# Batch 0's first k and v parts moved to ScalarE's DMA queue, and the last unit's products put into another order of banks and stores

## The chip, the cores and the metric

The kernel runs on one core of one Trainium2 chip. The metric is the device time of one execution in microseconds (us); the median of several executions is quoted. A *profile* is one execution taken by the hardware profiler; its *span* is some 1.8 us shorter than the device time of the same execution. PE is the TensorE matmul, PEld its weight load, DVE the VectorE, ACT the ScalarE, POOL the GpSimd and SP the SyncE.

Two kinds of number appear, and they must not be mixed. The *timed* numbers say what the change is worth. The *profiled* ones say where the time goes; each is one execution.

## The reference, cut to what matters

```python
q_p, k_p = phi(q), phi(k)                      # phi(x) = elu(x) + 1; q, k, v: 8 x 8 x 576 x 64, f32
kv  = einsum('bhsd,bhse->bhde', k_p, v)
out = einsum('bhsd,bhde->bhse', q_p, kv) / den # linear attention
x   = out as (4608, 512)
for e in range(4):                             # four experts, w1: 512 x 1024, w2: 1024 x 512, f32
    y += p[:, e:e+1] * (relu(x @ w1[e]) @ w2[e])
```

The kernel works in 36 units, nine tiles of 512 tokens by four experts. Eight tiles are one batch's first 512 tokens each; the ninth gathers the remaining 64 tokens (the *remainders*) of all batches. Most matmuls use a Strassen-like scheme with seven products where eight would be needed.

## The kernel before: the parts that matter

All of batch 0's loads are issued by SyncE, in one order. A part is 256 KB; `load_left` issues a remainder as two DMAs of 64 KB.

```python
ORDER = [(n, 2 * g + i) for g in range(2) for n in "qkv" for i in range(2)]
...
homes = ["h"] * 4 + [None] * NRAW + ["u2", "u3"]
for (n, i), home in zip(ORDER, homes):
    b0.load(n, i, home=home)                # q0 q1 k0 k1 [k rest] v0 v1 [v rest] q2 q3 k2 k3 v2 v3
    if i == 1 and n != "q":
        b0.load_left(n)
load_probs(nc.sync, True)
```

POOL issues the expert weights. In its program order that comes after the cast of the v remainder (`'lv'`), and part of it after a piece of phi of k3 (`'kd3'`):

```python
"START": (11, 'qa0', 'ka0', 'kd0', 'qa1', 'lka', 'qd0', 'lv', 6, ..., 'dma0', ..., 'kd3', ..., 'dma1', ...)
```

The last unit of all computes seven products, each for two blocks of 128 tokens, into two PSUM banks (`b` as `run`, `e` as `side`), and DVE adds each result to an accumulator. Product 3 needs POOL's last hidden sum:

```python
order = L2ORD if n < len(units) - 1 else (2, 1, 5, 6, 3, 7, 4)   # banks: e b e b e b b
...
if (j, e) == (NTILES - 1, E - 1):
    if p in (3, 7, 4):       # 3: whole rows of block i; 7 and 4: the two halves of block 2 + i
        store(j, ns, {3: slice(0, Dm), 7: c2, 4: c1}[p], True)
```

A store is two DMAs, one on SyncE's and one on ScalarE's queue, so this is six stores on each.

## Time and profile before

| what | value |
|---|---|
| time, median | 499.92 us (4 runs, 499.61 to 500.02) |
| profiled span | 498.2 us |
| PE busy | 97% of the span |
| batch 0's hardware-queue packets | 3.42 MB, from 1.85 to 14.56 us |
| POOL issues the first weights | 10.76 us |
| first store to the end of the span | 490.99 to 498.18 us |

The page, the parts on busy time and on the chain that ended last:

```profile
PE 483.7 (97%) x4343; PEld 408.5 (82%) x4343; DVE 378.1 (76%) x800; ACT 337.3 (68%) x680; POOL 357.5 (72%) x339
PE 83%; ACT 6%; DVE 4%; DMA 3%; POOL 1%; issue 1%; POOLq 0%; SPq 0%; ACTq 0%; DVEq 0%
```

In the middle PE is the limit, and neither half of the change touches the middle. Two places are left. The first is the start. The windows view gives, for each stretch, busy us and count of each engine, then the granted clock, the DMA share and GB/s:

```profile
core 0: us, PE busy (x) PEld busy (x) DVE busy (x) ACT busy (x) POOL busy (x), PEclk, DMA share, GB/s
2.00:6.00 4.00, 4.00 (x12) 1.49 (x11) 0.49 (x1) 0.65 (x2) 1.91 (x1) 1.00 0.97 289
6.00:10.00 4.00, 3.52 (x21) 1.51 (x18) 2.94 (x9) 3.48 (x7) 0.00 (x0) 1.00 0.89 270
13.00:20.00 7.00, 6.29 (x63) 3.89 (x61) 6.35 (x21) 5.72 (x15) 6.98 (x9) 1.00 1.35 187
26.00:34.00 8.00, 6.51 (x35) 2.99 (x34) 2.72 (x5) 3.35 (x6) 2.86 (x4) 1.00 1.14 218
```

The DMA engines are occupied from 2 us on, first by batch 0, then by weights. Between 26 and 34 us PE is busy for only 6.51 of 8 us. The view of waits of that stretch says why (waited for in total, times, longest):

```profile
DVE s L603 <- DMA w<-in_moe_w_dram: 9.2, 1, 9.2
PEld L731 <- DMA w<-in_moe_w_dram: 2.0, 2, 1.5
PE pe L731 <- DMA w<-in_moe_w_dram: 1.0, 1, 1.0
```

In the timeline these four lines tell the story of the start (start us, duration, engine, line, operation; in brackets the idle time before and what ended it):

```profile
7.70 0.40 ACT L353 ACTIVATE el<-rl 128x256 f16<-128x256 f32 x1
10.21 0.40 POOL L357 CAST vl<-rl 128x256 f16<-128x256 f32 x1 [4.67 <-DMA rl<-in_v_dram]
10.76 3.34 POOL L182 DMA_DIRECT2D w<-in_moe_w_dram  x4 [0.15 <-issue]
33.57 0.61 PE L731 MATMUL pb<-tt,s 128*128 128x256 f16 x4 [0.43 <-DVE s L605]
```

They are the exp of the k remainder, the cast of the v remainder, the first weight issue, and the first product that uses DVE's sum of weights. The last is a milestone that I call M.

The second place is the tail:

```profile
489.56 1.33 PE L666 MATMUL pe<-w,hs 128*128 128x256 f16 x8
490.05 0.55 PEld L666 LDWEIGHTS <-hs 128*128 128x128 f16 x6 [0.39 <-POOL hs L639]
490.99 3.77 SPq L555 DMA_DIRECT2D out_dram<-acc  x6
491.00 4.35 ACTq L555 DMA_DIRECT2D out_dram<-acc  x6
492.53 0.92 DVE L568 SCALAR_TENSOR_TENSOR acc<-pb,p_sb,acc 128x256 f32<-128x256 f32 x2 [0.25 <-PE pb L666]
```

PE waits inside product 3 for POOL, the stores run back to back on both queues (a `q` after the engine's name marks issuing), and DVE's last pair of adds waits for PE.

### The profile page before, as it was taken

To read this page: it belongs to the slowest core of one execution; us is meant where nothing else is said; L and a number is where in the kernel's file an instruction comes from. 1 tells how busy PE (TensorE), PEld (TensorE's weight loads), DVE (VectorE), ACT (ScalarE), POOL (GpSimd) and SP (SyncE) were. 2 spreads that over 40 slices of the span, in tenths; PEclk is the share of its full clock that TensorE was granted. 3 is DMA by queue.
4 is the path that set the end of the run, shared out by engine and by line. 5 is a ranking of instruction groups with operands and counts; after the bars stand their busy time and mean duration, and the time that the engine had idled before them with its cause. 6 is when DMAs were issued, how large, how long until landed. Compare 5 with 4: busy or idle time off the path is not lost.

```text
span 498.2 us, 11603 instructions
## 1 busy us (share of the span) xinstructions
PE 483.7 (97%) x4343; PEld 408.5 (82%) x4343; DVE 378.1 (76%) x800; ACT 337.3 (68%) x680; POOL 357.5 (72%) x339
## 2 busy tenths in 40 slices
PE   8989989899999999999999999999999999999995
PEld 3546756789898989898989898989898888888884
DVE  5647898788876988598869886888687756775685
ACT  5857969974987488847894789568954565446530
POOL 3734304878977697769776977698669877987773
PEclk9999999999999999999999999999999999999999
DMA  8999974642454234632454245523231020002002
GB/s 244 200 215 246 271 150 124 207 113 57 109 167 128 62 95 144 157 75 76 142 167 84 57 153 147 101 52 95 86 79 29 5 94 1 1 1 86 1 1 86
DMA packets 81880, 53.65 MB, mean 108 GB/s; under 512 B 46176, under 2 KB 75360, under 8 KB 81824
## 3 DMA queue, kind: packets, MB, share of 16 engines
q1 hardware_dynamic: 71520, 41.12, 30.5%
q0 software_dynamic: 9824, 11.27, 12.1%
q8 instruction: 34, 0.56, 0.5%
q10 hardware_dynamic: 480, 0.52, 0.3%
q14 instruction: 22, 0.18, 0.1%
HBM read 45.16 MB, written 9.44 MB: 110 GB/s over the span
## 4 chain that ended last, share of the span: by engine, by line
PE 83%; ACT 6%; DVE 4%; DMA 3%; POOL 1%; issue 1%; POOLq 0%; SPq 0%; ACTq 0%; DVEq 0%
PE py L666 37%; PE pb L731 23%; PE pe L731 17%; DMA w<-in_moe_w_dram 3%; PE py L577 2%; PE psum_kv L423 1%; PE psum_nd L463 1%; DMA rawh<-in_k_dram 1%; ACT u L742 1%; ACT vp L330 1%; ACT psum_ee L314 1%; DVE t L622 1%; DVE h L715 1%; DVE acc L568 1%; ACT h L757 1%
## 5 line engine op out<-in xcount | busy, mean ns | idle before, releaser
L568 DVE SCALAR_TENSOR_TENSOR acc<-py,p_sb,acc 128x256 f32<-128x256 f32 (+1 forms) x382 | 182.6, 488 | 46.4 <-PE py L666 40.1
L715 DVE CUSTOM_DVE_ANT_0 h<-pe,u 128x512 f16<-128x512 f32 x140 | 96.3, 688 | 46.9 <-PE pe L731 25.4
L731 PEld LDWEIGHTS <-w 128*128 128x128 f16 x1120 | 108.6, 98 | 18.4 <-DMA w<-in_moe_w_dram 2.0
L633 POOL TENSOR_TENSOR hs<-h 128x512 f16<-128x512 f16 x64 | 74.3, 1160 | 56.1 <-DVE h L715 55.0
L666 PEld LDWEIGHTS <-h 128*128 128x128 f16 x1024 | 99.6, 98 | 12.8 <-issue 1.4
L666 PE MATMUL py<-w,h 128*128 128x256 f16 x744 | 106.4, 273 | 0.5 <-ACT acc L566 0.5
L742 ACT COPY u<-pb 128x512 f32<-128x512 f32 x140 | 82.7, 591 | 27.5 <-PE pb L731 26.3
L635 POOL TENSOR_TENSOR hs<-hs,h 128x512 f16<-128x512 f16 x64 | 73.9, 1155 | 27.7 <-PE py L666 25.1
L731 PEld LDWEIGHTS <-s 128*128 128x128 f16 x840 | 81.5, 98 | 13.4 <-issue 1.1
L731 PE MATMUL pb<-tt,w 128*128 128x256 f16 x560 | 84.1, 273 | 0.5 <-ACT u L742 0.5
L666 PEld LDWEIGHTS <-hs 128*128 128x128 f16 x768 | 74.3, 98 | 9.1 <-POOL hs L639 0.4
L639 POOL TENSOR_TENSOR hs<-h,hs 128x512 f16<-128x512 f16 x64 | 74.4, 1162 | 3.6 <-PE py L666 3.1
L666 PE MATMUL py<-t,hs 128*128 128x256 f16 x496 | 74.4, 273 | 0.0
L637 POOL TENSOR_TENSOR h<-h 128x512 f16<-128x512 f16 x64 | 74.4, 1162 | 0.0
L757 ACT ACTIVATE h<-pe 128x512 f16<-128x512 f32 x70 | 41.9, 598 | 47.1 <-PE pe L731 46.6
L751 ACT COPY pe<-pb 128x512 f32<-128x512 f32 x70 | 40.2, 574 | 41.4 <-PE pb L731 14.8
L775 ACT ACTIVATE h<-pb 128x512 f16<-128x512 f32 x70 | 41.9, 599 | 8.8 <-PE pb L731 8.7
L731 PE MATMUL pb<-tt,s 128*128 128x256 f16 x280 | 42.0, 273 | 0.4 <-DVE s L605 0.4
L731 PE MATMUL pe<-tt,s 128*128 128x256 f16 x280 | 42.0, 273 | 0.0
L731 PE MATMUL pe<-xT,w 128*128 128x256 f16 x248 | 37.2, 273 | 1.0 <-DMA w<-in_moe_w_dram 1.0
L731 PE MATMUL pe<-xT,s 128*128 128x256 f16 x248 | 37.2, 273 | 0.9 <-DVE h L715 0.9
L731 PE MATMUL pb<-xT,w 128*128 128x256 f16 x248 | 37.2, 273 | 0.1
(120 smaller groups left out, 607.6 us busy)
## 6 DMA issues: line engine op xcount, KB each, us to landing
out_dram<-acc SPq DMA_DIRECT2D x32, 256.0 KB, 2.5
w<-in_moe_w_dram POOLq DMA_DIRECT2D x14, 512.0 KB, 12.1
rawb<-in_v_dram SPq DMA_DIRECT2D x26, 256.0 KB, 2.7
rawb<-in_q_dram SPq DMA_DIRECT2D x26, 256.0 KB, 2.8
rawb<-in_k_dram SPq DMA_DIRECT2D x26, 256.0 KB, 3.2
w<-in_moe_w_dram POOLq DMA_DIRECT2D x4, 256.0 KB, 6.6
rawb<-in_k_dram POOLq DMA_DIRECT2D x4, 256.0 KB, 10.1
rl<-in_q_dram SPq DMA_DIRECT2D x16, 64.0 KB, 2.5
```

The source lines that it names most:

```text
L568: nc.vector.scalar_tensor_tensor(out=acc, in0=ps, scalar=pscal, in1=acc, op0=AO.mult, op1=AO.add)
L633: nc.gpsimd.tensor_tensor(out=hs[0], in0=a21, in1=a22, op=AO.add)
L635: nc.gpsimd.tensor_tensor(out=hs[1], in0=hs[0], in1=a11, op=AO.subtract)
L637: nc.gpsimd.tensor_tensor(out=a21, in0=a11, in1=a21, op=AO.subtract)
L639: nc.gpsimd.tensor_tensor(out=hs[3], in0=a12, in1=hs[1], op=AO.subtract)
L666: nc.tensor.matmul(out=ps, lhsT=lhsT(k), rhs=rhs[:, k], start=first and k == 0, stop=k == FH - 1, skip_group_check=True,)
L715: nc.vector._custom_dve(TENSOR_ADD_SAT, out=out, in0=ps, in1=u, s0=BIG, s1=0.0)
L731: nc.tensor.matmul(out=ps[:, kk], lhsT=lk(kc), rhs=rhs[:, kc], start=first and kk == 0 and kc == 0, stop=kc == 1, skip_group_check=True,)
L742: nc.scalar.copy(u, self.b)
L751: nc.scalar.copy(self.e5, self.b)
L757: nc.scalar.activation(self.h[:, :, 0, 0:NH], self.e5, AF.Relu)
L775: nc.scalar.activation(self.h[:, :, 1, 0:NH], self.b, AF.Relu)
```

## The change

The intent at the start is that q and k arrive side by side and SyncE gets to the later parts sooner. In the last unit it is to take PE's two gaps away: product 3 comes later, behind POOL's last sum, and successive products alternate between the banks, so that product 4 no longer waits for the bank that product 7 has just filled. The stores become four whole-row ones per queue. The diff, cut at `...`, without the parts that are not used (other placements that the list allows); the remarks after `#` are mine:

```diff
+    "B0": ('sq0', 'sq1', 'ak0', 'ak1', 'slk', 'av0', 'av1', 'slv', 'sq2', 'sq3', 'sk2', 'sk3', 'sv2', 'sv3'),
...
-        homes = ["h"] * 4 + [None] * NRAW + ["u2", "u3"]
+        homes = dict(sq0="h", sq1="h", sk0="h", ...)   # the same buffers, now by name
-        for (n, i), home in zip(ORDER, homes):
-            b0.load(n, i, home=home)
-            if i == 1 and n != "q":
-                b0.load_left(n)
+        for x in CFG["B0"]:                      # s: SyncE's queue, a: ScalarE's
+            eng = {"s": nc.sync, "a": nc.scalar, "p": nc.gpsimd}[x[0]]
+            if x[1] == "l":
+                b0.load_left(x[2], eng=eng)
+            else:
+                b0.load(x[1], int(x[2]), eng, homes.get(x))
...
         if (j, e) == (NTILES - 1, E - 1):
-            if p == 2:                           # the first product takes the two banks
+            if p == 1:
...
-        if (j, e) == (NTILES - 1, E - 1):
-            if p in (3, 7, 4):
-                store(j, ns, {3: slice(0, Dm), 7: c2, 4: c1}[p], True)
-        elif e == E - 1 and p in (3, 4):
-            store(j, ns)
+        if e == E - 1 and p in (3, 4):
+            store(j, ns, j == NTILES - 1)
...
-            order = L2ORD if n < len(units) - 1 else (2, 1, 5, 6, 3, 7, 4)
+            order = L2ORD
+            if n == len(units) - 1:
+                order, at = (1, 2, 6, 5, 7, 3, 4), at + NSLOT      # banks: b e b e b e b
```

More of the change, by code (lines that the diff above doesn't have):

```diff
@@ L544, in new_py, with store @@
         return ppm.tile([P, Dm], FP32, tag="py", bufs=2, name="py")
-    def store(j, ns, ds=slice(0, Dm), last=False):
-        acc = accs[j, ns][:, ds]
+    def store(j, ns, last=False):
+        acc = accs[j, ns]
         if j < B:
@@ L555, in store @@
                 (nc.scalar if last and u else nc.sync).dma_start(
-                    out=out_b[2 * ns + u, SM:S, ds],
+                    out=out_b[2 * ns + u, SM:S],
                     in_=acc[u * HP : (u + 1) * HP],
@@ L794, in unit @@
         return layer1(j, e, hT, phs) + layer2(j, e, hT)
-    ORDER = [(n, 2 * g + i) for g in range(2) for n in "qkv" for i in range(2)]
     def order_of(at):
@@ L870 @@
         b0.alloc_left()
-        homes = ["h"] * 4 + [None] * NRAW + ["u2", "u3"]
-        for (n, i), home in zip(ORDER, homes):
-            b0.load(n, i, home=home)
-            if i == 1 and n != "q":
-                b0.load_left(n)
+        homes = dict(sq0="h", sq1="h", sk0="h", sk1="h", ak0="h", ak1="h", pv0="hs1", pv1="hs1", sv2="u2", sv3="u3")
+        for x in CFG["B0"]:
[4 more added lines that the diff above has]
+                b0.load(x[1], int(x[2]), eng, homes.get(x))
         load_probs(nc.sync, True)
@@ L886 @@
             "lv": (b0.left_v, nc.gpsimd),
+            "V2": (b0.load, "v", 2, nc.gpsimd, "hs3"),
+            "V3": (b0.load, "v", 3, nc.gpsimd, "hs3"),
             "dma0": (load_first, 0, 4),
@@ L899, with gate @@
             steps[f"ph{i}"] = partial, i
+        dump = pconst.tile([P, 1], FP32, tag="dump", name="dump")
+        def gate(n, i):
+            nc.gpsimd.tensor_copy(out=dump, in_=b0.raw[n, i][:, 0, 0, 0:1])
+        for n in "qkv":
+            for i in range(4):
+                steps[f"g{n}{i}"] = gate, n, i
         turn["aps"] = list(CFG["APS"])
```

## The prediction

> **What bounds it.** PE is busy 97% (page, part 1) and heads the chain of waits with 83%. Only the ends are not PE-bound: between 30 and 34 us PE loses 1.4 us (windows) while DVE waits 9.2 us and PE 1.0 us for weights (view of waits), and after 490 us the kernel drains.
>
> *Start.* The hardware queue carries batch 0 from 2 to 14 us at 264-311 GB/s, DMA share 0.88-1.02 (windows); the software queue with the weights is saturated from 14 to past 34 us (share 1.1-1.4). SyncE issues a 256 KB part in 0.46 us, a 64 KB remainder in 0.6-0.75 (timeline). Landings, from what ended waits: q0 3.55, k0 6.10, v0/v1 9.5, v remainder 10.2. POOL waits 4.7 us for that remainder and issues weights only at 10.76.
>
> *Tail.* POOL's last sum ends at 489.99 and holds product 3 back by 0.39 us; product 4 reuses product 7's bank and waits 0.31 us (timeline). The last DVE add ends 493.45. But ScalarE's six stores run back to back from 491.00, 0.5-0.8 us each, the last issued at 494.87, 1.4 us after its data; SyncE's last at 494.22. Data moves until about 496.5; the span ends at 498.2.
>
> **What the change does.** Work is the same. Start: k0, k1, v0, v1 move to ScalarE (4 x 0.5 us of issue before its 1.28 us table load, so ready near 4.1 us). Estimates from 290 GB/s shared equally: q0 3.55 -> 4.1, k0 6.1 -> 4.3, k1 and q1 near 5.7, v0/v1 9.5 -> 8.9, v remainder 10.2 -> 8.3. So POOL issues weights up to 2 us earlier. The Trainium skill, "DMA: Bandwidth & Descriptors", section "Issuing engines are not separate DMA queues", says several issuers only save issue time, as the same 16 engines carry all; this trace agrees so far, with a share of 0.9-1.0 from 2 us on. So the wait for weights near 31 us shrinks only by the idle share of the first 12 us and a better overlap of two queues: 0.3-1.0 us. Against it, earlier weights interleave with k3, v2, v3, which may land 1 us later. Net start: 0.5 us gained (estimate).
>
> Tail: order 1,2,6,5,7,3,4 puts product 3 behind the last sum, and gives product 4 the bank freed longer before. Both PE gaps (0.39 + 0.31) go; last add near 492.9 (0.55 earlier). Eight half-row stores (64 KB) become four full-row ones (128 KB): four issues per queue, the last near 493.6 (estimate) instead of 494.87, but twice as large. The same 1.05 MB drains at about 285 GB/s from a start 0.6 us later. Net tail: 0.6 us gained.
>
> All of it is critical, but is 1.1 of 500 us. Predicted 498.7 us, eight times in ten between 497.7 and 499.9; faster by over 2%: 0.01, within 2%: 0.98, slower by over 2%: 0.01.
>
> **What would show it.** Two hardware queues in the first 10 us; first exp of k0 near 4.7 instead of 6.13; POOL's cast of the v remainder near 8.5 instead of 10.21; first weight issue near 9; PE's wait near 31 us shorter and earlier. Last unit: no PE gap before products 3 and 4, four stores a queue. Middle unchanged.
>
> **What would make it wrong.** The weight stream's end may not move (purely rate-bound), leaving the tail; late v2/v3 may stall PE near 16-20 us; SyncE may stall where a remainder's semaphore must come free first; full-row stores may land later than they are issued earlier; or two queues may run clearly faster together, giving 2 us.

## The result and the profile after

498.35 us median (498.26 to 498.93, 4 runs) against 499.92: 1.6 us less. The ratio is 0.9972 with a 95% interval of 0.9955 to 0.9989. Ratios here are the mean time of one kernel's fast runs over that of the other's of the same rounds, so not quite the ratio of the medians quoted. Below 2% it counts as the same speed, but it is clear of 1. Two more timings of the same code gave 0.9964 (0.9950 to 0.9978) and 0.9989 (0.9977 to 1.0000). The last interval touches 1. So 0.5 to 1.8 us is what the runs support. Executions in which one die ran at a lower clock are left out of the means.

The profiled execution was the slowest of the four, with a span of 497.2 us. The windows of the start:

```profile
core 0: us, PE busy (x) PEld busy (x) DVE busy (x) ACT busy (x) POOL busy (x), PEclk, DMA share, GB/s
2.00:6.00 4.00, 4.00 (x15) 1.64 (x14) 1.54 (x3) 2.85 (x4) 1.76 (x1) 1.00 1.00 323
6.00:10.00 4.00, 3.19 (x17) 1.22 (x15) 1.29 (x4) 1.30 (x4) 0.15 (x1) 1.00 1.16 270
13.00:20.00 7.00, 6.26 (x63) 3.92 (x60) 6.14 (x19) 6.64 (x17) 6.98 (x9) 1.00 1.33 183
26.00:34.00 8.00, 7.84 (x45) 4.12 (x43) 3.49 (x7) 4.78 (x9) 3.16 (x5) 1.00 1.15 217
```

Batch 0 moved faster at first (323 instead of 289 GB/s), and PE is now busy for 7.84 of the 8 us from 26 to 34. The view of waits there has no PE wait for weights any more, and DVE's is 2 us shorter:

```profile
DVE s L604 <- DMA w<-in_moe_w_dram: 7.2, 1, 7.2
PEld L729 <- DVE s L606: 0.3, 1, 0.3
```

The four lines of the story, by the timeline:

```profile
9.40 0.42 ACT L354 ACTIVATE el<-rl 128x256 f16<-128x256 f32 x1 [2.70 <-DMA rl<-in_k_dram]
10.01 0.40 POOL L358 CAST vl<-rl 128x256 f16<-128x256 f32 x1 [3.86 <-DMA rl<-in_v_dram]
10.57 3.39 POOL L183 DMA_DIRECT2D w<-in_moe_w_dram  x4 [0.16 <-issue]
32.80 0.61 PE L729 MATMUL pb<-tt,s 128*128 128x256 f16 x4
```

This is not what I had pictured. The remainders did not come earlier: k's exp is 1.7 us later, v's cast 0.2 us earlier. PE's attention work ends 1.19 us *later* than before. Yet M is 0.77 us earlier. The tail:

```profile
490.57 2.48 SPq L556 DMA_DIRECT2D out_dram<-acc  x4
490.58 2.84 ACTq L556 DMA_DIRECT2D out_dram<-acc  x4
490.94 0.92 DVE L569 SCALAR_TENSOR_TENSOR acc<-pb,p_sb,acc 128x256 f32<-128x256 f32 x2
```

The last pair of adds ends at 491.86, 1.59 us earlier, but the span ends only 1.01 us earlier. PE's instruction stream is the same in both kernels up to the last unit, so the two traces can be laid side by side, instruction by instruction. After minus before: 1.19 us later in the attention, 0.78 earlier at M, 0.55 from 48 us on, and exactly 1.00 from 152 us to the first product of the last unit. The jump of 0.45 near 151 us has nothing to do with any line that was changed. In the timeline of before it is this wait of PE, for ScalarE's first sum into an accumulator:

```profile
150.76 0.60 PE L731 MATMUL pb<-xT,w 128*128 128x256 f16 x4
151.84 0.60 PE L666 MATMUL py<-w,h 128*128 128x256 f16 x4 [0.47 <-ACT acc L566]
```

and after, where the gap is short and ScalarE's own wait is put down to the store that must free the accumulator:

```profile
150.31 0.47 ACT L567 ACTIVATE acc<-py,p_sb 128x256 f32<-128x256 f32 x1 [0.57 <-DMA out_dram<-acc]
150.84 0.60 PE L667 MATMUL py<-w,h 128*128 128x256 f16 x4
```

So the first pair of traces left three questions: is the gain the start's or the tail's, is the 0.45 us near 151 us part of it, and why is a later attention faster?

### The profile page after: what moved, and what is told of

The parts are those of the page before. It is cut to its first block, busy times and chain, and to the rows that moved or that the text cites. A ratio compares the mean times of both kernels' runs of the same rounds, so it can differ in the third digit from the quotient of the medians.

```text
span 497.2 us, 11596 instructions
## 1 busy us (share of the span) xinstructions
PE 482.3 (97%) x4343; PEld 408.8 (82%) x4343; DVE 378.2 (76%) x800; ACT 337.5 (68%) x680; POOL 358.0 (72%) x339
## 4 chain that ended last, share of the span: by engine, by line
PE 82%; DMA 7%; ACT 5%; DVE 3%; POOL 2%; issue 1%; SPq 0%; POOLq 0%; ACTq 0%
PE py L667 38%; PE pb L729 22%; PE pe L729 17%; DMA rawb<-in_k_dram 2%; DMA rl<-in_k_dram 2%; PE py L578 1%; PE psum_nd L464 1%; PE psum_kv L424 1%; DMA rl<-in_v_dram 1%; ACT psum_ee L315 1%; DVE acc L569 1%; ACT u L740 1%; DVE t L623 1%; DMA rawh<-in_q_dram 1%; POOL w L183 1%
## 5 line engine op out<-in xcount | busy, mean ns | idle before, releaser
L667 PE MATMUL py<-w,hs 128*128 128x256 f16 x248 | 37.2, 273 | 0.0
```

Source lines behind the costliest of these rows:

```text
L667: nc.tensor.matmul(out=ps, lhsT=lhsT(k), rhs=rhs[:, k], start=first and k == 0, stop=k == FH - 1, skip_group_check=True,)
```

## The experiments

Twelve runs, in three groups of four; the kernels of a group shared a chip and the runs of the kernel before. All results were correct.

| run | what it is | median us | before, same rounds | ratio (95%) |
|---|---|---|---|---|
| a1 | start alone | 498.36 | 500.06 | 0.9961 (0.9946-0.9976) |
| a2 | tail alone | 499.73 | 500.06 | 0.9992 (0.9977-1.0007) |
| a3 | changed kernel again | 498.41 | 500.06 | 0.9964 (0.9950-0.9978) |
| a4 | remainders first | 500.60 | 500.06 | 1.0005 (0.9989-1.0021) |
| b1 | weights issued early | 500.83 | 499.90 | 1.0020 (1.0006-1.0033) |
| b2 | changed, old stores | 498.03 | 499.90 | 0.9962 (0.9950-0.9975) |
| b3 | changed, old order | 497.98 | 499.90 | 0.9969 (0.9953-0.9986) |
| b4 | kernel before again | 499.58 | 499.90 | 0.9995 (0.9982-1.0009) |
| c1 | changed kernel, third time | 498.82 | 499.78 | 0.9989 (0.9977-1.0000) |
| c2 | as b2 | 498.53 | 499.78 | 0.9978 (0.9966-0.9989) |
| c3 | as b3 | 498.18 | 499.78 | 0.9983 (0.9964-1.0003) |
| c4 | changed, only k moved | 498.34 | 499.78 | 0.9977 (0.9965-0.9989) |

### a1 to a3: the halves apart

a1 is the changed kernel with before's order, banks and stores of the last unit; a2 is before with the new ones; a3 is the changed kernel once more.

```diff
 a1, from the changed kernel              a2, from the kernel before
-order, at = (1, 2, 6, 5, 7, 3, 4), ...   -(2, 1, 5, 6, 3, 7, 4)
+order = (2, 1, 5, 6, 3, 7, 4)            +(1, 2, 6, 5, 7, 3, 4), bank pair taken at product 1
-store(j, ns, j == NTILES - 1)            -store(j, ns, {3: ..., 7: c2, 4: c1}[p], True)
+store(j, ns, {3: ..., 7: c2, 4: c1}[p], True)  +store(j, ns, j == NTILES - 1)
```

> Only the queues of batch 0's loads change; the last unit is as before. Theory A (the gain is mostly at the start: the two queues together move batch 0 about 11% faster, so the weight stream begins and ends earlier): 0.8 to 1.2 us less than before, PE 0.7 to 0.9 us earlier at 33 us though the attention is 1.2 us later. Theory B (the gain is mostly the tail, and the 0.5 us that the first trace shows near 150 us is chance): 0.3 to 0.6 us less.

> Only the last unit changes (order, banks, full-row stores). Theory A: the last DVE add comes 0.59 us earlier in its unit, but the stores also begin 0.6 us later, so the end moves by 0 to 0.3 us. Theory B: 0.6 to 1.0 us less than before.

> The changed kernel once more beside its two halves: 1.3 to 1.7 us less than before. If the halves add up, start plus tail should give this within 0.3 us. The profile tells whether the 0.46 us near 150 us, which the first trace showed as gained, is gained again.

Measured: 498.36 for the start alone, 498.41 for both, on the same chip. The tail alone is not told apart from before (0.9992, interval across 1). Theory A holds and B falls: the start has the whole gain, and more than the 0.8 to 1.2 us expected by the medians (1.7). a2's profile shows both sides of the tail. Its last add comes 6.80 us after the unit's first product, where before's comes 7.39 us after it, as expected 0.59 earlier; yet from the first product to the end of the span it is 12.12 us, and 12.11 before.

### b4: was the wait near 151 us chance?

> The kernel before once more, with a profile: 0 +- 0.3 us. It tells whether the wait of 0.46 us at PE near 150 us belongs to that kernel or to one execution: by chance, it is gone or shorter here, and the profiled span is then 0.4 to 0.6 us below the first one's 498.2.

The code is the kernel before, unchanged. Its time is 499.58, its profiled span 497.4 instead of 498.2, and the gap is gone:

```profile
150.67 0.60 PE L731 MATMUL pb<-xT,w 128*128 128x256 f16 x4
151.11 0.60 PE L666 MATMUL py<-w,h 128*128 128x256 f16 x4
```

So 0.45 of the 1.00 us by which the first pair of profiles differed ahead of the last unit was one execution's luck. In c2, a variant of the *changed* kernel, PE's gap at the same instruction is 0.40 us, and none is left in a1 or a2. This is why I give M and the last unit as means of several profiles. M is 33.57, 33.47 and 33.69 us in the three profiles with before's start (before, b4, a2), mean 33.58. In the eight with the new start (after, a1, a3, b2, b3, c1, c2, c3) it is 32.32 to 32.80, mean 32.45. That is 1.13 us. The last unit's first product differs by 1.06 us over the same profiles (485.65 and 484.59). What is gained at M arrives at the end.

### c4: how much has to be moved?

```diff
-"B0": ('sq0', 'sq1', 'ak0', 'ak1', 'slk', 'av0', 'av1', 'slv', 'sq2', ...
+"B0": ('sq0', 'sq1', 'ak0', 'ak1', 'slk', 'sv0', 'sv1', 'slv', 'sq2', ...
```

> The changed kernel with v0 and v1 back on SyncE's queue, so that only k0 and k1 go by ScalarE. Theory A (the gain is what the two queues together save in draining batch 0): about half of the overlap remains, the last hardware packet comes near 13.6 us, PE at 33 us is 0.4 to 0.7 us ahead of before instead of 1.0, and the time is 0.3 to 0.6 us above the changed kernel. Rival (the gain is k0 and k1 landing early, so ScalarE and DVE start sooner): no loss, within 0.2 us of the changed kernel.

Theory A, in the form "so much overlap, so much gain", fell: with half as much on ScalarE's queue nothing is lost. 498.34 stands against 498.82 for the changed kernel on the same chip, and M is 32.23. The last packet of batch 0 comes at 13.08 us, where half the gain would have given 13.6. The rival guessed the time but not the reason. k0 and k1 do land early in both kernels. But the attention is 0.6 us earlier than in the first profile of before here and 0.7 to 1.2 us later in the changed kernel, and the time hardly tells. Here PE waits for weights again, as it did in before, only sooner:

```profile
PEld L729 <- DMA w<-in_moe_w_dram: 1.0, 1, 1.0
PEld L729 <- DVE s L606: 0.9, 1, 0.9
```

So M is not set by the same thing in the two kernels. Measure it from N, the start of the attention's last four products `psum_nd`. Here are N in before, in the changed kernel and in c4, and then M in c4:

```profile
18.19 0.39 PE L463 MATMUL psum_nd<-kvz,qT 128*128 128x130 f16 x4 [0.23 <-ACT kvz L439]
19.38 0.39 PE L464 MATMUL psum_nd<-kvz,qT 128*128 128x130 f16 x4 [0.32 <-ACT kvz L440]
17.59 0.39 PE L464 MATMUL psum_nd<-kvz,qT 128*128 128x130 f16 x4 [0.33 <-ACT kvz L440]
32.23 0.61 PE L729 MATMUL pb<-tt,s 128*128 128x256 f16 x4 [0.43 <-DVE s L606]
```

From N to M it takes 15.38 to 15.84 us in the three profiles with before's start, 14.64 in c4, and 13.39 to 13.50 in the eight with the changed start. In a4, below, where PE waits for nothing on the way, it takes 13.40. So waiting for weights cost before 2.0 to 2.4 us, costs c4 1.2 and the changed kernel at most 0.1. The changed kernel is no longer held up by weights at M: its late attention sets M and gives back a part of what the earlier weights won. That c4 and the changed kernel come out so close is in part chance.

What the two kernels share is the end of batch 0's hardware packets: 14.56, 14.09 and 14.27 us in the three profiles with before's start, 13.14 to 13.68 in the eight with the changed start, 13.08 here. The first megabyte of weights, as the packets count it, is complete at 19.09 to 19.53, at 18.01 to 18.74, and at 17.98 us.

c4 also points to what delayed the attention. With v0 and v1 behind the k remainder on SyncE's queue, its exp starts at 6.96 us; with them on ScalarE's, at 8.88 to 9.40. In the changed kernel, in the single microsecond from 6 to 7, the DMA view reads:

```profile
q10 hardware_dynamic: 222, 0.22, 80.3%
q1 hardware_dynamic: 253, 0.06, 30.8%
```

q10 is ScalarE's queue, q1 SyncE's (packets, MB, share of 16 engines' time). In this microsecond the counts are alike, as if the two queues took turns packet by packet. But SyncE's packets were the remainders' small ones, so it moved 0.06 MB against 0.22. Equal turns are shown for this microsecond only: in the one before SyncE's queue moved 93 packets and ScalarE's 283, in the one after 675 and 84.

### a4: the remainders first

```diff
-"B0": ('sq0', 'sq1', 'ak0', 'ak1', 'slk', 'av0', 'av1', 'slv', 'sq2', ...
+"B0": ('sq0', 'ak0', 'slk', 'slv', 'ak1', 'sq1', 'av0', 'av1', 'sq2', ...
```

> The changed kernel with both remainders issued right after the first q part, q1 behind k1. Theory S (the 64 KB remainders with their 256-byte packets are starved beside ScalarE's 1 KB packets): POOL's cast of the v remainder moves from 10.0 to 6 to 8 us, weights are issued 2 us earlier, the k remainder's exp moves from 9.4 to about 7. If the weight stream is bound by its rate and total, its end moves by less than 0.3 us and the time stays within 0.3 us of the changed kernel; if it is bound by when it is first issued, the time falls by another 1 to 2 us.

A miss that taught something: 500.60 us, 2.2 more than the changed kernel on the same chip. The v remainder's cast came at 8.80 us (6 to 8 expected), so POOL issued the first weights at 9.14 instead of 10.1 to 10.6. The first weight packet moved at 13.03 us all the same, just when batch 0 was through (last packet 13.31). Issuing earlier bought nothing. Taken alone this looks as if the weights had to wait for batch 0; b1, below, refutes that. On the other side q1 now stood behind the remainders in SyncE's queue, and SyncE issued it at 5.65 us, after gaps of 0.8 and 0.9 us in its issuing, where the program has it wait for earlier DMAs whose semaphores it uses again. Its first use on ScalarE came at 9.30 us, after 4.00 us of waiting for it; the k remainder's exp, which follows it there, came at 10.36 (about 7 expected), and PE's attention was 2.36 us later than in before. Now PE was the limit at M, not the weights:

```profile
33.95 0.60 PE L729 MATMUL pb<-tt,s 128*128 128x256 f16 x4
```

No wait of PE for weights is left between 26 and 34 us. Once the weights no longer hold PE up, each further delay of the attention arrives at M in full: a4's attention is 1.17 us later than that of the first profile of the changed kernel, and its M 1.15 us later.

### b1: the weights issued before the v remainder

```diff
-"START": (..., 'qd0', 'lv', 6, ..., 'ka2', 'dma0', 2, 'qT2', ...
+"START": (..., 'qd0', 'dma0', 'lv', 6, ..., 'ka2', 2, 'qT2', ...
```

> The changed kernel, but POOL issues its first four weight parts before it waits for the v remainder, so near 6.2 us instead of 10.2 to 10.6. Theory P (the weight stream does not get going until batch 0's hardware queues have drained, whenever it is issued): the first weight packets still move near 12.6 to 13 us, and the time stays within 0.4 us of the changed kernel. Theory R (all queues take turns at the packets): weight packets move from about 8.5 us, batch 0 lands about 1 us later, and the weights' fourth megabyte comes up to 1 us earlier or later than 32.5 to 33.0.

Neither theory as written. POOL issued at 6.15 us and weight packets moved from 9.66 us, so they do not wait for the hardware queues to drain (theory P falls). But nor did they share evenly at first. From 10 to 12 us:

```profile
q0 software_dynamic: 676, 0.34, 124.6%
q1 hardware_dynamic: 95, 0.09, 15.7%
```

Theory R's equal turns are seen only from about 12 us on (for instance 166 and 171 packets between 12 and 13). Batch 0's last packet came at 18.51 us instead of 13.3. The first megabyte of weights was complete at 18.59 us, no earlier than in the changed kernel (18.10 to 18.74). Then POOL waited for k3 before it could issue more:

```profile
15.44 2.00 POOL L327 TENSOR_SCALAR kp<-rawb 128x512 f16<-128x512 f32 x1 [5.12 <-DMA rawb<-in_k_dram]
```

The fifth weight part was issued at 17.40 us (15.95 in the changed kernel), M slid to 34.14 and the time to 500.83. Most of the slide is the attention's, whose loads now landed later: N is 20.41 us, 1.03 later than in the first profile of the changed kernel, and from N to M it takes 13.73 us. Starting the weights 3 us sooner gained nothing, because the DMA engines were already full: from 10 to 12 us their share was 1.40, and they moved 214 GB/s where the changed kernel moved 344.

### b2, b3, c1 to c3: order and stores apart

b2 and c2 are the changed kernel with before's six half-row stores. b3 and c3 are the changed kernel with before's order and banks, and four whole-row stores.

```diff
 b2, c2: stores as in before                       b3, c3: order and banks as in before
-if e == E - 1 and p in (3, 4): store(...)         -order, at = (1, 2, 6, 5, 7, 3, 4), at + NSLOT
+if p in (3, 7, 4): store(j, ns, {...}[p], True)   +order = (2, 1, 5, 6, 3, 7, 4)
```

> The changed kernel with before's half-row stores: new order and banks, six stores a queue, product 7's half stored first. Theory D (the tail ends when the stores have drained, not when the last add ends): the last add stays 0.5 to 0.6 us earlier in its unit than in before, the first store issue comes 0.3 us earlier than product 3's, and the last landing comes 3.9 to 4.4 us after the last add; the time is within 0.3 us of the changed kernel. If the last add alone counted, the time would be 0.5 us below the kernel with the start alone.

> The changed kernel with before's order and banks in the last unit, but full-row stores, four a queue. Theory D: first store issue as early as in before (product 3 is ready sooner), last landing about 3.3 to 3.6 us after the last add, time within 0.3 us of the changed kernel, perhaps 0.2 us better. If the last add alone counted: 0.5 us slower than the changed kernel.

> The changed kernel again, as the yardstick for the other three on the same chip: 1.4 to 1.9 us less than before; batch 0's hardware packets end near 13.2 to 13.7 us.

> The changed kernel with before's six half-row stores a queue. Its first timing was 498.03 on another chip. If that was the kernel and not the chip, its spans are 0.3 to 0.5 us below the changed kernel's, because its first store is issued 0.3 us sooner in the last unit and the last landing comes 3.7 us after the last add instead of 4.2; if the chip, within 0.2 us.

> The changed kernel with before's order and banks of the last unit and four full-row stores a queue. Same question: 0.3 to 0.5 us below the changed kernel in the span if the first timing (497.98) was the kernel, within 0.2 us if it was the chip. Theory D either way: the last add comes 0.6 us later than in the changed kernel, and the end does not.

From the profiles, in us. U is the start of the last unit's first product, F the first store's issue, A the end of the last add, E the end of the span; in brackets the number of profiles:

| last unit | U to F | U to A | F to E | U to E |
|---|---|---|---|---|
| old order, six half-row stores (before, b4, a1) | 4.93-4.95 | 7.38-7.40 | 7.16-7.27 | 12.11-12.20 |
| new order, four whole-row stores (after, a2, a3, c1) | 5.52 | 6.80 | 6.59-6.65 | 12.10-12.17 |
| new order, six half-row stores (b2, c2) | 4.64 | 6.80 | 7.26-7.35 | 11.90-11.99 |
| old order, four whole-row stores (b3, c3) | 4.94 | 7.39 | 6.72-6.78 | 11.65-11.72 |

The columns separate cleanly. The last add depends on the order alone, and the end does not follow it: the old order has the later add and, with whole rows, the earliest end. From the first store's issue to the end it takes about 7.2 us with six stores a queue and 6.6 to 6.8 with four, whatever the order. So the tail is a string of stores. In these four variants it is set by when the string begins and how many stores it has. The changed kernel shortens the string by 0.6 us and begins it 0.6 us later, since product 3, whose result is stored first, was moved back. Theory D holds. Its landing times were a little off: the last store landed 3.6 to 3.7 us after the last add in b2 and c2 (3.9 to 4.4 expected for b2), and 3.2 in b3 and c3 (3.3 to 3.6 expected for b3).

b3's stores, to be compared with those of before and after above:

```profile
489.60 3.17 SPq L556 DMA_DIRECT2D out_dram<-acc  x4
```

The 3.17 us contain a pause of 0.85 us before the third store, whose sum was not ready, and the last store is issued 0.15 us after the last add. So in b3 the arithmetic has a part in the end again.

Keeping the whole-row stores and leaving the order alone would thus save 0.4 us of U to E. In the timed runs this is only hinted at. b3 and c3 have medians of 497.98 and 498.18, below c1's 498.82 and a3's 498.41. But each had an execution at 500.44 or 501.07, and their ratios (0.9969, 0.9983) overlap with the changed kernel's. The expected span gain of 0.3 to 0.5 us was met by medians for c3 (spans 496.4 against c1's 497.0) and c2 (496.7). I call it likely, not shown. c1's own expectation (1.4 to 1.9 us below before) was missed: it is 0.96 below by the medians, though batch 0's packets ended at 13.22 us as expected. c4's load order with b3's tail was not run.

## Why the prediction was right, point by point

The time was forecast as 498.7 (497.7 to 499.9) and measured as 498.35; a gain of 1.1 us was forecast and 1.6 measured. The number held, but as a sum of two terms that were off in opposite directions.

1. **What bounds the start: right.** The wait for weights near 31 us was on the path. It went away, and M moved until the attention, now later, set it.
2. **"Net start: 0.5 us gained": mis-sized.** It measured 1.13 us at M and 1.06 us at the last unit, means over three and eight profiles. The term that was too small is the wait for weights: it was to shrink by 0.3 to 1.0 us, taken from the Trainium skill ("DMA: Bandwidth & Descriptors", section "Issuing engines are not separate DMA queues"), that several issuers save only issue time. It shrank by about 2 us (N to M), and the later attention took about half of that back. Batch 0's hardware packets ended about 1 us earlier. Issue time alone was not what held before up: by 8 us SyncE had issued 2.36 MB of batch 0, and 1.69 MB had moved.
3. **"v remainder 10.2 -> 8.3", "weights up to 2 us earlier": wrong.** The cast came at 10.01 and the issue at 10.57. The estimate shared the rate equally by bytes, but while the remainders were moved, SyncE's queue got much less than half of the bytes (0.06 against 0.22 MB from 6 to 7 us), their packets being small. It did no harm, because the issue time of weights was not what bound them: a4 issued at 9.14 and b1 at 6.15 without gaining anything.
4. **q0 at 4.1 and k0's exp near 4.7: right.** ScalarE ran both exps back to back from 4.18 to 5.33 us.
5. **The risk "late v2/v3 may stall PE": half right.** PE's attention was later by 0.7 to 1.2 us, but with the k remainder, as c4 makes likely, and not with v2 or v3. It stayed below the 2.0 to 2.4 us that waiting for weights had cost, so M still came earlier, but only by the difference. In a4, at 2.36 us, nothing was left. Another risk on the list came true too: SyncE issued nothing from 6.59 to 8.21 us, waiting for a k remainder. No run shows what that cost.
6. **"Net tail: 0.6 us gained": wrong, it is 0.0.** The last add came 0.59 us earlier (0.55 forecast), and PE's two gaps did go. The failing step was to count that gain at all, and in the same paragraph to note that the same 1.05 MB drains "from a start 0.6 us later". The later start is the term that counted; it cancelled the 0.6 us that fewer stores saved.
7. **"Middle unchanged": right for the code, not for the pair of profiles.** 0.45 us of their difference came from a wait that the kernel before shows in one execution and not in the next.

What stays open: why SyncE's queue alone moved batch 0 at 279 to 295 GB/s between 2 and 6 us, and the two queues with the changed start at 321 to 332. The DMA share was near 1 in both. More load on the second queue is not the reason, as c4 shows. Nor can it be the two queues side by side alone: from 10 to 12 us SyncE's queue was alone in all these profiles and moved 344 to 349 GB/s with the changed start, but 268 to 311 with before's. No run put the parts in another order on SyncE's queue alone, so how much of the gain belongs to the second queue, and how much to the order in which the parts arrive, is not shown.

## What to carry to other kernels

When DMA engines are full, ask when the *sum* of what must be moved is through, not when a transfer is issued: issuing the weights 4 us sooner won nothing, and moving two 256 KB parts to a second queue won about 1 us. When a wait is gone, ask what sets the pace next: here it was the attention, which the same change had delayed. At the end of a kernel, look for the string of stores: to bring forward the last arithmetic pays only if the first store is not put back by it. And before a difference of half a us between two profiles is explained, profile the unchanged kernel once more.

## What the Trainium skill lacked or had wrong

- "DMA: Bandwidth & Descriptors", section "Issuing engines are not separate DMA queues", and the rule in "Rules for kernel authors" that spreading DMAs over SP, ACT and GpSimd for bandwidth does not help: here batch 0's 3.42 MB ended at 13.1 to 13.7 us with two hardware queues and at 14.1 to 14.6 with one, from the same first packet at 1.85 us. The kernel gained about 1 us by it. Whether it is the second queue that does it, or the order of the parts that came with it, no run separates.
- Same page, "Queues, rings and completion order", on turns between queues at packet granularity: it agrees for two hardware queues in one us (222 and 253 packets) but not in its neighbours (283 and 93, 84 and 675); whether the packets that the profile counts are what the page calls packets is not shown. The page could add what this us shows, that a queue of small packets gets a small share of the bytes (0.06 against 0.22 MB). Between the software queue and a hardware queue it was uneven at first (676 and 95 packets in 2 us), even later (166 and 171 in 1 us).
- No page that I used gives the cost of a string of stores at a kernel's end: from the first issue to the end of the span, 7.2 us for six a queue and 6.6 to 6.8 us for four with the same 1.05 MB.
